# Attention and a multiplicative FFN on one Trainium2 core: q by 128 partitions with a tail, xT by pairs of batches, and x transposed by DMA from pair 10 on

## The chip, the core and the metric

The kernel runs on one core of a Trainium2 chip. A core has five engines that work side by side, each with its own in-order queue: TensorE (matmuls; PE in the profile, with its weight loads as PEld), VectorE (DVE), ScalarE (ACT), GpSimd (POOL) and SyncE (SP). Transfers and DMA transposes run on 16 DMA engines; an engine only issues them, and the issue stands in that engine's queue. The metric is device time in microseconds (us), less is better.

## The reference

Two stages, in float32 outside, for 8 batches, 8 heads, 1152 positions and head size 64:

```python
q_pool = q.reshape(B, H, S // factor, factor, D).mean(axis=3)      # factor 2: 576 queries a head
scores = scale * np.matmul(q_pool, k.transpose(0, 1, 3, 2))
attn = softmax(scores)                                             # over 1152 keys
x = (attn @ v).transpose(0, 2, 1, 3).reshape(B * 576, 512)         # 4608 tokens of 8 heads x 64
a = x @ w1                                                         # 512 x 1024
b = x @ w2
out = ((a * b) @ w3) @ w_out                                       # 1024 x 1024, 1024 x 512
```

Order of queries within a head is free inside the kernel, as long as each output row lands in its place.

## The kernel before

**Pairs.** Two heads of one batch are worked together as a pair; there are 32 pairs, four a batch. For each pair k, v and q are loaded in float32 (`load_kq`, L175, and `load_v`, L183). `cast_kq` (L189) makes 16-bit k on POOL and adds neighbouring queries (L198) on POOL too (on DVE for pair 0). q lies on 96 partitions by 6 queries each (`QP`, `QC`), k on 128 by 9.

**Turning k and q.** The scores need k and q with the head size on partitions. For pairs 0 to 7 `transp_pe` (L215) does it on TensorE: six transposes of q (L221), nine of k (L224), and three copies out on DVE. From pair 8 on `transp` (L207) issues two DMA transposes on SyncE (L210 for k into `kT2`, L212 for q into `qpT`).

**Scores and exponentials.** Keys by queries of a pair are a flat row of 9 x 576 columns, and all pairs form one long row, cut in 324 pieces of 512 columns. `scores` (L231) makes a piece for both heads with matmuls on L240 into one of three PSUM buffers `psc`, and ScalarE puts its exponential into a ring in SBUF (L245).

**Attention times v, and x.** A pair's queries are five tiles of 128 (the last one overlaps the one before by 64, `TO`). `av_pair` (L252) multiplies the ring by v with a column of ones for the sum: 18 matmuls (L259) into `avb`. `av_norm` (L274) takes the reciprocal (L276) and scales (L284) on DVE. The FFN needs x with features on partitions (`xT`, a ring of 5 batches of 576 tokens). For pairs below `XD` = 20 each tile is turned on TensorE (`x_turn`, L289, one transpose) and copied out by DVE (`x_copy`, L296); this happens one tile later, right behind the next tile's L259. From pair 20 on the five tiles are kept in `xb5`, and `x_dma` (L265) issues two DMA transposes on SyncE (L269 for four tiles, L271 for the last 64 queries).

**FFN.** The tokens are cut in 9 chunks of 512. w3 and w_out are first multiplied into one matrix (`t_groups`). `moe_groups` (L358) then gives a chunk 16 projections (L345, four matmuls of 512 columns each, alternately w1 and w2, with DVE multiplying the two on L370) and four output groups (L377, eight matmuls). The outputs are scaled and stored by `store` (L348), on POOL's queue while attention runs and on SyncE's after it. As positions in a chunk are tokens in 96-blocks, one group of 128 rows goes out in two or more transfers. The very last group is `go_last` (L393): it makes its 512 columns in two halves (L399), each scaled on ScalarE (L401), and is stored from ScalarE's queue.

**The order.** It is written out by the loop at L510 and nothing reorders it on an engine. A visit is three pieces of scores, one or two attention-value steps, and up to two FFN groups taken from a queue of chunks (`fill`): two projections or one output group with one step, one projection with two steps. There are 108 visits. At a pair's first piece the k and q transposes of the next pair are issued (`transp`) and the pair after that is prepared (`prepare`, L457: cast, then loads on SyncE's queue for pairs from 8 on, on POOL's before). A chunk enters the queue when its last x tile is there: `done_at` (L475) tells the attention-value step after which that is. For tiles turned on TensorE that is at once. For those turned by DMA the chunk is held until `HELD` = 5 steps past the end of the pair (L497). After the visits the remaining chunks are worked in the order in which they became ready, with ScalarE taking a part of the copies (`tail`).

Of the kernel before, what the change touches and what calls it, by code (L numbers as in the profile page):

```python
# [23 lines left out]
def _general(tc, q, k, v, out, w1sb, w2sb, T16):  # L24
# [8 lines left out]
    NF = dff // 128  # L33
    QP = 96
    QC = Sq // QP
    SCALE = 0.5 * float(D) ** -0.5
# [3 lines left out]
    with tc.tile_pool(name="gen", bufs=1) as sb, \  # L40
# [3 lines left out]
        for h in range(H):  # L44
# [70 lines left out]
def kernel(  # L115
# [20 lines left out]
    HP = H // 2  # L136
# [2 lines left out]
    G = 512  # L139
    NS = NP * FLAT // G  # L140
    RING = 24 * Sq
    QP = 96
    QC = Sq // QP
    E1 = D + 1
    SCALE = 0.5 * float(D) ** -0.5
    SCL = 16.0
    TO = [0, 128, 256, 384, Sq - 128]
    NT5 = len(TO)
# [6 lines left out]
    att = fast.enter_context(tc.tile_pool(name="att", bufs=2))  # L155
# [3 lines left out]
    ident16 = const.tile([128, 128], FP16)  # L159
# [13 lines left out]
    kq, vs, pairs = {}, {}, {}  # L173

    def load_kq(p, k_eng, q_eng):  # L175
        b, h0 = p // HP, 2 * (p % HP)
        kst = att.tile([128, 2, NJ * D], FP32, tag="kst")
        k_eng.dma_start(out=kst, in_=k[b, h0:h0 + 2].rearrange("u (p c) d -> p u (c d)", p=128))
        qst = att.tile([QP, 2, QC * 2 * D], FP32, tag="qst")
        q_eng.dma_start(out=qst, in_=q[b, h0:h0 + 2].rearrange("u (p c) d -> p u (c d)", p=QP))  # L180
        kq[p] = (kst, qst)

    def load_v(p, eng):  # L183
        b, h0 = p // HP, 2 * (p % HP)
# [2 lines left out]
        vs[p] = vst  # L187

    def cast_kq(p):  # L189
        kst, qst = kq.pop(p)  # L190
# [3 lines left out]
        qs = att.tile([QP, QC, 2, D], FP16, tag="qs")  # L194
        qv = qst.rearrange("p u (c t d) -> p u c t d", t=2, d=D)
        eng = nc.vector if p == 0 else nc.gpsimd
        for u in range(2):
            eng.tensor_tensor(out=qs[:, :, u, :], in0=qv[:, u, :, 0, :], in1=qv[:, u, :, 1, :], op=ALU.add)  # L198
        pairs[p] = [kpair, qs]

    def cast_v(p):
        va = vaugs[p % NVA]
# [2 lines left out]
        nc.gpsimd.tensor_copy(out=va[:, :, :, 0:D], in_=vs.pop(p).rearrange("p u (c d) -> p u c d", d=D))  # L205

    def transp(p):  # L207
        kpair, qs = pairs[p]
        kT2 = att.tile([128, NJ, 128], FP16, tag="kT2", bufs=3)
        nc.sync.dma_start(out=kT2, in_=kpair.rearrange("p c u d -> p (c u d)"), transpose=True)  # L210
        qpT = att.tile([128, QC, QP], FP16, tag="qpT", bufs=3)
        nc.sync.dma_start(out=qpT, in_=qs.rearrange("p c u d -> p (c u d)"), transpose=True)  # L212
        pairs[p] = (kT2, qpT.rearrange("p c i -> p (c i)"))

    def transp_pe(p):  # L215
        kpair, qs = pairs[p]
        kT2 = att.tile([128, NJ, 128], FP16, tag="kT2", bufs=3)
        qpT = att.tile([128, QC, QP], FP16, tag="qpT", bufs=3)
# [6 lines left out]
        nc.vector.tensor_copy(out=qpT.rearrange("p c i -> p (c i)"), in_=pt[:, 0:Sq])  # L225
        nc.vector.tensor_copy(out=kT2[:, 0:3].rearrange("p c i -> p (c i)"), in_=pt[:, Sq:Sq + 384])
        nc.vector.tensor_copy(out=kT2[:, 3:NJ].rearrange("p c i -> p (c i)"), in_=pt[:, 1024:1024 + (NJ - 3) * 128])  # L227
        pairs[p] = (kT2, qpT.rearrange("p c i -> p (c i)"))


    def scores(s):  # L231
# [16 lines left out]
    XR = 5 * Sq  # L248
    xT = att.tile([128, NC, XR], FP16, tag="xT", bufs=1)
    xbts = {}  # L250

    def av_pair(i):  # L252
        p, t = i // NT5, i % NT5
        va = vaugs[p % NVA]
        o = (i % 3) * 2 * E1
        for jt in range(NJ):
            c0 = ((p * NJ + jt) * Sq) % RING + TO[t]
            for u in range(2):
                nc.tensor.matmul(avb[:, o + u * E1:o + u * E1 + E1], ring[:, u, c0:c0 + 128], va[:, u, jt, :],  # L259
                                 start=(jt == 0 and u == 0), stop=(jt == NJ - 1), skip_group_check=True)  # L260

    XD = 20
    xb5 = {}

    def x_dma(p):  # L265
        b, hp = p // HP, p % HP
        c0 = (b * Sq) % XR
        xb = xb5.pop(p)
        nc.sync.dma_start(out=xT[:, hp, c0:c0 + 512].rearrange("p (t i) -> p t i", i=128),  # L269
                          in_=xb[:, 0:4].rearrange("p t u d -> p (t u d)"), transpose=True)  # L270
        nc.sync.dma_start(out=xT[:, hp, c0 + 512:c0 + Sq],  # L271
                          in_=xb[Sq - 512:128, 4].rearrange("p u d -> p (u d)"), transpose=True)
# [61 lines left out]
    CH = 512  # L334
# [23 lines left out]
    def moe_groups(c):  # L358
        gT = msb.tile([128, NF, CH], FP16, tag="g8", bufs=2, name="gT")
# [76 lines left out]
    def w_load(dst, src):  # L436
# [7 lines left out]
        out=ident16, in_=ident16, compare_op=ALU.not_equal, fill=1.0,  # L444
# [172 lines left out]
```

## Time and profile before

| | |
|---|---|
| median of 3 runs | 430.56 us (430.50 to 430.72) |
| profiled execution, its time | 430.84 us |
| its span, first to last instruction | 428.8 us |
| TensorE clock granted | 0.998 of full |
| TensorE busy | 408.0 us, 95% of the span |
| ScalarE busy | 326.7 us, 76% |
| VectorE busy | 205.5 us, 48% |
| GpSimd busy | 178.7 us, 42% |
| DMA moved | 84.59 MB in 79537 packets, 53489 of them under 512 B |
| attention's visits | about 11 to 350 us; the FFN alone after 364 us |

Groups in the profile have the line of the kernel, the engine, the operation, what it writes and reads, how often, then busy time and mean duration of one in ns, then the engine's idle time just before them and what ended most of it. Durations of matmuls are longer than their spacing, since they overlap in the array; starts are what to subtract. An engine with a "q" behind its name (SPq, POOLq, ACTq) is its queue issuing a transfer. The chain is the work that ended last, followed back from the end of the kernel.

### The profile page before, as it was taken

To read this page: it belongs to the slowest core of one execution; us is meant where nothing else is said; L and a number is where in the kernel's file an instruction comes from. 1 tells how busy PE (TensorE), PEld (TensorE's weight loads), DVE (VectorE), ACT (ScalarE), POOL (GpSimd) and SP (SyncE) were. 2 spreads that over 40 slices of the span, in tenths; PEclk is the share of its full clock that TensorE was granted. 3 is DMA by queue.
4 is the path that set the end of the run, shared out by engine and by line. 5 is a ranking of instruction groups with operands and counts; after the bars stand their busy time and mean duration, and the time that the engine had idled before them with its cause. 6 is when DMAs were issued, how large, how long until landed. Compare 5 with 4: busy or idle time off the path is not lost.

```text
span 428.8 us, 12736 instructions
## 1 busy us (share of the span) xinstructions
PE 408.0 (95%) x5317; PEld 251.2 (59%) x5317; DVE 205.5 (48%) x626; ACT 326.7 (76%) x359; POOL 178.7 (42%) x215
## 2 busy tenths in 40 slices
PE   1799999999999999999999999999999999999993
PEld 1376666666565656665666656665677856444442
DVE  1144564666356554655465635554445536534330
ACT  1889788889988988999889998999999980232221
POOL 3776755744675317630684218431861021000000
PEclk9999999999999999999999999999999999999999
DMA  8999999999999996999699949999795023030303
GB/s 254 250 262 264 251 232 229 264 230 239 276 296 289 256 216 205 278 232 270 178 252 280 307 100 240 254 252 240 216 205 108 15 64 69 10 99 0 99 1 105
DMA packets 79537, 84.59 MB, mean 197 GB/s; under 512 B 53489, under 2 KB 54513, under 8 KB 79473
## 3 DMA queue, kind: packets, MB, share of 16 engines
q1 hardware_dynamic: 70080, 56.57, 57.0%
q0 software_dynamic: 8544, 25.11, 23.7%
q10 hardware_dynamic: 848, 2.03, 1.7%
q8 instruction: 43, 0.70, 0.7%
q14 instruction: 22, 0.17, 0.1%
HBM read 67.11 MB, written 9.44 MB: 179 GB/s over the span
## 4 chain that ended last, share of the span: by engine, by line
PE 92%; DVE 3%; ACT 2%; DMA 2%; issue 0%; POOL 0%; ACTq 0%
PE avb L259 21%; PE psc L240 18%; PE mot L345 16%; PE mo L345 14%; PE mo L377 10%; PE mot L377 5%; PE mo L324 3%; ACT ring L245 2%; DMA kst<-in_k_dram 2%; PE avb L289 1%; PE ptk L224 1%; PE ptk L221 1%; DVE qpT L225 1%; PE mol L399 0%; PE mot L324 0%; DVE kT L227 0%
## 5 line engine op out<-in xcount | busy, mean ns | idle before, releaser
L245 ACT ACTIVATE ring<-psc 128x1024 f16<-128x1024 f32 x324 | 308.0, 1025 | 41.7 <-PE psc L240 38.7
L259 PEld LDWEIGHTS <-ring 128*128 128x128 f16 x2880 | 104.4, 98 | 36.5 <-issue 11.8
L259 PE MATMUL avb<-vaug,ring 128*128 128x65 f16 x2880 | 114.1, 193 | 2.1 <-DVE xT L296 1.4
L240 PE MATMUL psc<-qpT,kT 64*128 64x512 f16 (+7 forms) x1152 | 94.9, 291 | 2.8 <-ACT ring L245 1.8
L355 POOL DMA_DIRECT2D out_dram<-osb x48 | 25.1, 526 | 105.9 <-DVE rzall L276 105.8
L198 POOL TENSOR_TENSOR qs<-qst 96x384 f16<-96x384 f32 x62 | 60.5, 996 | 13.9 <-DMA qst<-in_q_dram 12.4
L240 PEld LDWEIGHTS <-kT 64*128 64x128 f16 x1152 | 45.5, 95 | 29.6 <-issue 6.1
L192 POOL CAST kpair<-kst 128x1152 f16<-128x1152 f32 x32 | 37.1, 1158 | 53.0 <-DMA kT<-kpair 22.5
L276 DVE RECIPROCAL rzall<-avb 128x2 f32<-128x2 f32 x160 | 26.6, 166 | 46.3 <-PE avb L289 30.8
L345 PEld LDWEIGHTS <-w2sb 128*128 128x128 f16 x320 | 28.6, 97 | 27.0 <-issue 2.8
L345 PEld LDWEIGHTS <-w1sb 128*128 128x128 f16 x320 | 28.4, 98 | 27.3 <-issue 3.4
L377 PEld LDWEIGHTS <-gT 128*128 128x128 f16 x280 | 25.5, 98 | 31.2 <-issue 4.0
L377 PE MATMUL mo<-T,gT 128*128 128x512 f16 x184 | 43.7, 380 | 0.0
L345 PE MATMUL mot<-xT,w2sb 128*128 128x512 f16 (+2 forms) x172 | 41.1, 364 | 0.0
L370 DVE TENSOR_TENSOR gT<-mot,asb 128x512 f16<-128x512 f32 x40 | 27.7, 692 | 24.2 <-PE mot L345 24.2
L205 POOL CAST vaug<-vst 128x1152 f16<-128x1152 f32 x32 | 36.6, 1145 | 6.1 <-DMA vst<-in_v_dram 6.0
L345 PE MATMUL mot<-xT,w1sb 128*128 128x512 f16 (+2 forms) x152 | 38.0, 373 | 0.0
L365 ACT COPY asb<-mot 128x512 f32<-128x512 f32 x21 | 12.3, 586 | 32.6 <-PE mot L345 32.6
L345 PE MATMUL mo<-xT,w1sb 128*128 128x512 f16 (+2 forms) x168 | 36.1, 344 | 0.0
L390 DVE TENSOR_SCALAR osb<-mo 128x512 f32<-128x512 f32 x23 | 15.9, 692 | 42.1 <-PE mo L377 42.1
L367 DVE COPY asb<-mo 128x512 f32<-128x512 f32 x35 | 24.2, 691 | 23.7 <-PE mo L345 23.7
L345 PE MATMUL mo<-xT,w2sb 128*128 128x512 f16 (+2 forms) x148 | 33.0, 351 | 0.0
(57 smaller groups left out, 266.8 us busy)
## 6 DMA issues: line engine op xcount, KB each, us to landing
vst<-in_v_dram SPq DMA_DIRECT2D x25, 576.0 KB, 6.2
kst<-in_k_dram SPq DMA_DIRECT2D x23, 576.0 KB, 6.9
qst<-in_q_dram SPq DMA_DIRECT2D x22, 576.0 KB, 8.1
kst<-in_k_dram POOLq DMA_DIRECT2D x8, 576.0 KB, 11.9
qst<-in_q_dram POOLq DMA_DIRECT2D x8, 576.0 KB, 13.6
vst<-in_v_dram POOLq DMA_DIRECT2D x7, 576.0 KB, 7.8
out_dram<-osb POOLq DMA_DIRECT2D x16, 192.0 KB, 3.4
w3c<-in_moe_w_dram POOLq DMA_DIRECT2D x4, 512.0 KB, 9.2
```

Of the source, the lines that this page charges most:

```text
L192: nc.gpsimd.tensor_copy(out=kpair.rearrange("p c u d -> p u c d"), in_=kst.rearrange("p u (c d) -> p u c d", d=D))
L198: eng.tensor_tensor(out=qs[:, :, u, :], in0=qv[:, u, :, 0, :], in1=qv[:, u, :, 1, :], op=ALU.add)
L205: nc.gpsimd.tensor_copy(out=va[:, :, :, 0:D], in_=vs.pop(p).rearrange("p u (c d) -> p u c d", d=D))
L240: nc.tensor.matmul(psc[:, u, f - s * G:f - s * G + ln], kT2[u * 64:u * 64 + 64, jt, :], qpT[u * 64:u * 64 + 64, i0:i0 + ln], start=True, s ...
L245: nc.scalar.activation(out=ring[:, :, r0:r0 + G], in_=psc, func=AF.Exp, bias=0.0, scale=SCALE)
L259: nc.tensor.matmul(avb[:, o + u * E1:o + u * E1 + E1], ring[:, u, c0:c0 + 128], va[:, u, jt, :], start=(jt == 0 and u == 0), stop=(jt == N ...
L276: nc.vector.reciprocal(out=rzall[:, i, :], in_=av[:, :, D:E1].rearrange("p u o -> p (u o)"))
L345: nc.tensor.matmul(pw[:, d0:d0 + n], wt[:, mc, ft * 128:ft * 128 + 128], xT[:, mc, a:a + n], start=(mc == 0 and d0 == 0), stop=(mc == NC - ...
L355: eng.dma_start(out=dst, in_=osb[r:r + n, :])
L367: nc.vector.tensor_copy(out=asb, in_=pa)
L370: nc.vector.tensor_tensor(out=gT[:, ft, :], in0=pb, in1=asb, op=ALU.mult)
L377: nc.tensor.matmul(po, gT[:, ft, tt:tt + 128], T16[:, ft, :], start=(ft == 0), stop=(ft == NF - 1))
```

## The change

Three things, which hang together by the block size of 128:

- q of a pair is loaded as 128 partitions by 4 queries (`qst`) plus the last 64 queries on 64 partitions (`qtl`), in two transfers; it is added in two instructions, and turned in 4 + 1 transposes on TensorE (pairs 0 to 7) or by two DMA transposes (from pair 8 on).
- `xT` holds the batches two by two: 4 blocks of 128 of the even batch, the 64 last queries of both side by side, 4 blocks of 128 of the odd batch (`xpos`). A group of 128 output rows is then one block of one batch, stored in one transfer, or the two tails, stored in two. Which step a chunk waits for follows from `xpos`.
- `XD` is 10 instead of 20: x of pairs 10 to 19 is turned by DMA too.

```diff
-    QP = 96
-    QC = Sq // QP
+    QM = 4
+    QT = Sq - QM * 128
...
-        qst = att.tile([QP, 2, QC * 2 * D], FP32, tag="qst")
-        q_eng.dma_start(out=qst, in_=q[b, h0:h0 + 2].rearrange("u (p c) d -> p u (c d)", p=QP))
+        qst = att.tile([128, 2, QM * 2 * D], FP32, tag="qst")
+        qtl = att.tile([QT, 2, 2 * D], FP32, tag="qtl")
+        q_eng.dma_start(out=qst, in_=q[b, h0:h0 + 2, 0:QM * 256].rearrange("u (p c) d -> p u (c d)", p=128))
+        q_eng.dma_start(out=qtl, in_=q[b, h0:h0 + 2, QM * 256:S].rearrange("u (p t) d -> p u (t d)", t=2))
...
-        for u in range(2):
-            eng.tensor_tensor(out=qs[:, :, u, :], in0=qv[:, u, :, 0, :], in1=qv[:, u, :, 1, :], op=ALU.add)
+        eng.tensor_tensor(out=qs.rearrange("p c u d -> p u c d"), in0=qv[:, :, :, 0], in1=qv[:, :, :, 1], op=ALU.add)
+        eng.tensor_tensor(out=qt, in0=qtl[:, :, 0:D], in1=qtl[:, :, D:2 * D], op=ALU.add)
...
-        qpT = att.tile([128, QC, QP], FP16, tag="qpT", bufs=3)
-        nc.sync.dma_start(out=qpT, in_=qs.rearrange("p c u d -> p (c u d)"), transpose=True)
+        qpT = att.tile([128, Sq], FP16, tag="qpT", bufs=3)
+        nc.sync.dma_start(out=qpT[:, 0:QM * 128].rearrange("p (c i) -> p c i", i=128),
+                          in_=qs.rearrange("p c u d -> p (c u d)"), transpose=True)
+        nc.sync.dma_start(out=qpT[:, QM * 128:Sq], in_=qt.rearrange("p u d -> p (u d)"), transpose=True)
...
-        for c in range(QC):
-            nc.tensor.transpose(pt[:, c * QP:c * QP + QP], qs[:, c].rearrange("p u d -> p (u d)"), ident16[0:QP, 0:QP])
+        for c in range(QM):
+            nc.tensor.transpose(pt[:, c * 128:c * 128 + 128], qs[:, c].rearrange("p u d -> p (u d)"), ident16)
+        nc.tensor.transpose(pt[:, QM * 128:Sq], qt.rearrange("p u d -> p (u d)"), ident16[0:QT, 0:QT])
...
+    def xpos(b, t):
+        if b % 2 == 0:
+            return b * Sq + t * 128
+        return b * Sq + (QT + t * 128 if t < QM else 0)
...
-    XD = 20
+    XD = 10
...
+        c0 = xpos(b, 0) % XR
+        nc.sync.dma_start(out=xT[:, hp, c0:c0 + QM * 128].rearrange("p (t i) -> p t i", i=128),
+                          in_=xb[:, 0:QM].rearrange("p t u d -> p (t u d)"), transpose=True)
+        c0 = xpos(b, QM) % XR
+        nc.sync.dma_start(out=xT[:, hp, c0:c0 + QT],
+                          in_=xb[128 - QT:128, QM].rearrange("p u d -> p (u d)"), transpose=True)
...
     def store(eng, pos, osb):
-        r = 0
-        while r < 128:
-            b, a = (pos + r) // Sq, (pos + r) % Sq
-            cc, p0 = a // QP, a % QP
-            n = min(QP - p0, 128 - r)
-            dst = out[b * Sq:b * Sq + Sq, :].rearrange("(p c) n -> p c n", c=QC)[p0:p0 + n, cc, :]
-            eng.dma_start(out=dst, in_=osb[r:r + n, :])
-            r += n
+        b, r = pos // (2 * Sq) * 2, pos % (2 * Sq)
+        if r == QM * 128:
+            for u in range(2):
+                r0 = (b + u) * Sq + QM * 128
+                eng.dma_start(out=out[r0:r0 + QT, :], in_=osb[u * QT:u * QT + QT, :])
+            return
+        if r > QM * 128:
+            b, r = b + 1, r - QM * 128 - 2 * QT
+        eng.dma_start(out=out[b * Sq:b * Sq + QM * 128, :].rearrange("(p c) n -> p c n", c=QM)[:, r // 128, :], in_=osb)
...
-        b, r = ((c + 1) * CH - 1) // Sq, ((c + 1) * CH - 1) % Sq
-        done_at.setdefault((b * HP + HP - 1) * NT5 + min(r // 128, NT5 - 1), []).append(c)
+        last = max((b * HP + HP - 1) * NT5 + t for b in range(B) for t in range(NT5)
+                   if xpos(b, t) < (c + 1) * CH and xpos(b, t) + (128 if t < QM else QT) > c * CH)
+        done_at.setdefault(last, []).append(c)
```

By this the last step that a chunk waits for moves by 1 to 4 steps for chunks 1, 3, 5 and 7 (chunk 7 now waits for the last tile of the last pair), and chunk 8 becomes ready one step earlier than chunk 7, so that the two change places in the order.

More of the change, by code (lines that the diff above doesn't have):

```diff
@@ L178, in load_kq @@
         k_eng.dma_start(out=kst, in_=k[b, h0:h0 + 2].rearrange("u (p c) d -> p u (c d)", p=128))
-        qst = att.tile([QP, 2, QC * 2 * D], FP32, tag="qst")
-        q_eng.dma_start(out=qst, in_=q[b, h0:h0 + 2].rearrange("u (p c) d -> p u (c d)", p=QP))
-        kq[p] = (kst, qst)
+        qst = att.tile([128, 2, QM * 2 * D], FP32, tag="qst")
+        qtl = att.tile([QT, 2, 2 * D], FP32, tag="qtl")
+        q_eng.dma_start(out=qst, in_=q[b, h0:h0 + 2, 0:QM * 256].rearrange("u (p c) d -> p u (c d)", p=128))
+        q_eng.dma_start(out=qtl, in_=q[b, h0:h0 + 2, QM * 256:S].rearrange("u (p t) d -> p u (t d)", t=2))
+        kq[p] = (kst, qst, qtl)
     def load_v(p, eng):
@@ L189, in cast_kq @@
     def cast_kq(p):
-        kst, qst = kq.pop(p)
+        kst, qst, qtl = kq.pop(p)
         kpair = att.tile([128, NJ, 2, D], FP16, tag="kpair")
@@ L193, in cast_kq @@
                               in_=kst.rearrange("p u (c d) -> p u c d", d=D))
-        qs = att.tile([QP, QC, 2, D], FP16, tag="qs")
+        qs = att.tile([128, QM, 2, D], FP16, tag="qs")
+        qt = att.tile([QT, 2, D], FP16, tag="qt")
         qv = qst.rearrange("p u (c t d) -> p u c t d", t=2, d=D)
         eng = nc.vector if p == 0 else nc.gpsimd
-        for u in range(2):
-            eng.tensor_tensor(out=qs[:, :, u, :], in0=qv[:, u, :, 0, :], in1=qv[:, u, :, 1, :], op=ALU.add)
-        pairs[p] = [kpair, qs]
+        eng.tensor_tensor(out=qs.rearrange("p c u d -> p u c d"), in0=qv[:, :, :, 0], in1=qv[:, :, :, 1], op=ALU.add)
+        eng.tensor_tensor(out=qt, in0=qtl[:, :, 0:D], in1=qtl[:, :, D:2 * D], op=ALU.add)
+        pairs[p] = [kpair, qs, qt]
     def cast_v(p):
@@ L207, in transp @@
     def transp(p):
-        kpair, qs = pairs[p]
+        kpair, qs, qt = pairs[p]
         kT2 = att.tile([128, NJ, 128], FP16, tag="kT2", bufs=3)
         nc.sync.dma_start(out=kT2, in_=kpair.rearrange("p c u d -> p (c u d)"), transpose=True)
-        qpT = att.tile([128, QC, QP], FP16, tag="qpT", bufs=3)
-        nc.sync.dma_start(out=qpT, in_=qs.rearrange("p c u d -> p (c u d)"), transpose=True)
-        pairs[p] = (kT2, qpT.rearrange("p c i -> p (c i)"))
+        qpT = att.tile([128, Sq], FP16, tag="qpT", bufs=3)
+        nc.sync.dma_start(out=qpT[:, 0:QM * 128].rearrange("p (c i) -> p c i", i=128),
+                          in_=qs.rearrange("p c u d -> p (c u d)"), transpose=True)
+        nc.sync.dma_start(out=qpT[:, QM * 128:Sq], in_=qt.rearrange("p u d -> p (u d)"), transpose=True)
+        pairs[p] = (kT2, qpT)
     def transp_pe(p):
-        kpair, qs = pairs[p]
+        kpair, qs, qt = pairs[p]
         kT2 = att.tile([128, NJ, 128], FP16, tag="kT2", bufs=3)
-        qpT = att.tile([128, QC, QP], FP16, tag="qpT", bufs=3)
+        qpT = att.tile([128, Sq], FP16, tag="qpT", bufs=3)
         pt = ps.tile([128, 2, 512], FP32, tag="psc", bufs=3, name="ptk").rearrange("p b c -> p (b c)").bitcast(FP16)
-        for c in range(QC):
-            nc.tensor.transpose(pt[:, c * QP:c * QP + QP], qs[:, c].rearrange("p u d -> p (u d)"), ident16[0:QP, 0:QP])
+        for c in range(QM):
+            nc.tensor.transpose(pt[:, c * 128:c * 128 + 128], qs[:, c].rearrange("p u d -> p (u d)"), ident16)
+        nc.tensor.transpose(pt[:, QM * 128:Sq], qt.rearrange("p u d -> p (u d)"), ident16[0:QT, 0:QT])
         cols = [Sq + c * 128 if c < 3 else 1024 + (c - 3) * 128 for c in range(NJ)]
@@ L224, in transp_pe @@
             nc.tensor.transpose(pt[:, cols[c]:cols[c] + 128], kpair[:, c].rearrange("p u d -> p (u d)"), ident16)
-        nc.vector.tensor_copy(out=qpT.rearrange("p c i -> p (c i)"), in_=pt[:, 0:Sq])
+        nc.vector.tensor_copy(out=qpT, in_=pt[:, 0:Sq])
         nc.vector.tensor_copy(out=kT2[:, 0:3].rearrange("p c i -> p (c i)"), in_=pt[:, Sq:Sq + 384])
         nc.vector.tensor_copy(out=kT2[:, 3:NJ].rearrange("p c i -> p (c i)"), in_=pt[:, 1024:1024 + (NJ - 3) * 128])
-        pairs[p] = (kT2, qpT.rearrange("p c i -> p (c i)"))
+        pairs[p] = (kT2, qpT)
     def scores(s):
@@ L266, in x_dma @@
         b, hp = p // HP, p % HP
-        c0 = (b * Sq) % XR
         xb = xb5.pop(p)
[L269 to L272, printed above, removed]
+        c0 = xpos(b, 0) % XR
[4 more added lines that the diff above has]
+                          in_=xb[128 - QT:128, QM].rearrange("p u d -> p (u d)"), transpose=True)
     def av_norm(i):
@@ L293, in x_copy @@
         b, hp = p // HP, p % HP
-        r0 = 0 if t < NT5 - 1 else NT5 * 128 - Sq
-        c0 = (b * Sq + TO[t] + r0) % XR
+        r0 = 0 if t < QM else 128 - QT
+        c0 = xpos(b, t) % XR
         nc.vector.tensor_copy(out=xT[:, hp, c0:c0 + 128 - r0], in_=xpt[:, r0:128])
```

## The prediction

> **What bounds the kernel now.** I read the page's busy times and chain first, then the rows by operation, then the order in time on TensorE, on SyncE and at the end.
>
> ```profile
> span 428.8 us, 12736 instructions
> ...
> PE 408.0 (95%) x5317; PEld 251.2 (59%) x5317; DVE 205.5 (48%) x626; ACT 326.7 (76%) x359; POOL 178.7 (42%) x215
> ...
> PE 92%; DVE 3%; ACT 2%; DMA 2%; issue 0%; POOL 0%; ACTq 0%
> ...
> L245 ACT ACTIVATE ring<-psc 128x1024 f16<-128x1024 f32 x324 | 308.0, 1025 | 41.7 <-PE psc L240 38.7
> ```
>
> TensorE carries 92% of the chain. ScalarE waits for it (38.7 us), but not by much: its 324 exponentials take 308.0 us, 0.95 us each, so a visit of three has a floor of 2.85 us. Both must be looked at visit by visit. First a visit while x is still turned on TensorE, then one after, both with two attention-value steps (V) and one projection (f):
>
> ```profile
> 167.16 0.83 PE L240 MATMUL psc<-qpT,kT 64*128 64x512 f16 x10
> 167.94 0.71 PE L259 MATMUL avb<-vaug,ring 128*128 128x65 f16 x18
> 168.49 0.22 PE L289 MATMUL avb<-ident,xbt 128*128 128x128 f16 x1
> 168.54 1.03 PE L345 MATMUL mo<-xT,w1sb 128*128 128x512 f16 x4
> 169.43 0.72 PE L259 MATMUL avb<-vaug,ring 128*128 128x65 f16 x18
> 169.99 0.22 PE L289 MATMUL avb<-ident,xbt 128*128 128x128 f16 x1
> 170.14 0.26 PE L240 MATMUL psc<-qpT,kT 64*128 64x192 f16 x2
> ```
>
> ```profile
> 270.74 0.87 PE L240 MATMUL psc<-qpT,kT 64*128 64x512 f16 x10
> 271.54 0.72 PE L259 MATMUL avb<-vaug,ring 128*128 128x65 f16 x18
> 272.10 1.02 PE L345 MATMUL mo<-xT,w1sb 128*128 128x512 f16 x4
> 272.96 0.71 PE L259 MATMUL avb<-vaug,ring 128*128 128x65 f16 x18
> 273.61 0.26 PE L240 MATMUL psc<-qpT,kT 64*128 64x192 f16 x2
> ```
>
> Columns: start, duration. From first score to first score: 170.14 - 167.16 = 2.98 us with two transposes (L289), 273.61 - 270.74 = 2.87 without. So before, this kernel already shows the state that the change extends: its visits from pair 20 on.
>
> **The change, part by part.** Sums are against the profiled execution: 430.84 us, of which 428.8 is span; the median of the three runs, 430.56, is 0.28 lower. No change that can be told is within 0.2%, 0.86 us.
>
> 1. *x by DMA from pair 10.* Fifty transposes on L289 and fifty copies on L296 go, in visits 39 to 71 (I number visits by three scores each). An L289 costs TensorE less than its 0.22 us, since matmuls overlap: in the rows above an L259 group's start lies 0.71 us ahead of the next score with L289 between (169.43 to 170.14) and 0.65 without (272.96 to 273.61). So it adds 0.06, and 50 x 0.06 = 3.0 us is the most if nothing else limits. I read it from whole visits: VfV takes 2.96 us early (17 visits, 2.95 to 2.98) and 2.88 late; two projections and one V 3.20 and 3.19; an output group (L377) and one V 3.20 and 3.155; with two V 3.81 and 3.69. Visits 39 to 71 are 14, 11, 5 and 3 of these: 14 x 0.084 + 11 x 0.016 + 5 x 0.045 + 3 x 0.125 = 1.96. Bounds -3.0 and -1.2 (only the VfV visits gain); I take **-2.0**, because late visits are the same instructions. The DVE copies cost nothing (DVE 48% busy).
>
> 2. *A later start of a chunk.* Chunk 2 was ready right after its last transpose; with DMA it is held until five V steps past the pair's end. By the order of issue that the code gives, visit 48 then finds no projection, and up to visit 71 two are done less (14 VfV, 10 with two projections and one V, 6 and 2 with an output group, and one empty); they come back in visits 90 and 105, one more each. A visit with two V and nothing else stood in the trace before:
>
> ```profile
> 67.77 0.83 PE L240 MATMUL psc<-qpT,kT 64*128 64x384 f16 x10
> ...
> 70.73 0.39 PE L240 MATMUL psc<-qpT,kT 64*128 64x512 f16 x2
> ```
>
> 2.96 us, as long as with a projection. So visit 48 saves almost nothing against a VfV; I give it the floor of 2.85. The visits to 71 then sum to 14 x 2.88 + 10 x 3.19 + 6 x 3.155 + 2 x 3.69 + 2.85 = 101.4 us, 0.8 below the 102.1 that term 1 leaves (104.1 - 2.0). Two projections of four matmuls, 0.216 us each, come later at full price, 1.73: **+0.9**. Bounds: +0.2 if TensorE ran through the empty visit (0.78 + 2 x 0.65 us), +1.0 by the row above.
>
> 3. *The end.* Chunk 8 now becomes ready one step before chunk 7 and is worked first. The split last group (`go_last`, L399) keys on chunk 8, so it moves into the middle and the kernel ends with an ordinary group of chunk 7.
>
> ```profile
> 419.96 1.04 PE L399 MATMUL mol<-T,gT 128*128 128x256 f16 x8
> 421.51 1.03 PE L399 MATMUL mol<-T,gT 128*128 128x256 f16 x8 [0.52 <-ACT osb L401]
> ```
>
> In the middle it holds TensorE 419.96 to 422.4, 2.42 us, against 8 x 0.216 = 1.73: +0.69. At the end, before: last store issued on ACT's queue at 423.40, landed 3.2 later, 6.6 us after the group's start. An ordinary group of chunk 6 starts at 378.51, its second store is issued at 381.74 and lands in 2.0: 5.2 us. So -1.35, net **-0.7**. Bounds: +0.7 (stores no earlier) and -1.4 (no wait in the middle).
>
> 4. *q.* On TensorE's pairs 0 to 7, six transposes of 96 columns (0.042 us warm, 0.080 in pairs 0 and 1) become four of 128 (0.056 and 0.107 by L224) and one of 64: at most **+0.15** in all. POOL: two adds of 996 ns for 384 elements become one of 512 and one of 128: by elements 1.33 + 0.33, from above 2.0, so -0.3 or 0 a pair; and an issue more of some 0.65 us in pairs 2 to 9. Nothing: k of pairs 3 to 7 is cast 8 us or more before its transposes. If that were gone, TensorE would wait for each late us. At the start, ACT's queue issues qst, qtl, then the next k; q landed at 6.79, the adds ended 7.83, six transposes were done 0.34 us before k's (8.90). qtl's bytes were part of qst's, so I take 0; if it landed only with the next k, 10.7, the start would move 2 us. Stores: 27 instead of 48 on POOL, 13 instead of 24 in the tail, hidden.
>
> 5. *SyncE's queue and the DMAs.* Each pair from 10 to 19 adds two transposes (1.2 and 1.12 us of SyncE's time); each from 8 on a q tail's transpose (about 1.1 by the 64-row one of x), each load of q one more issue (0.33). The tightest place is the transposes of pair 16, which now stand behind x of pair 12:
>
> ```profile
> 168.97 1.50 SPq L210 DMA_TRANSPOSE kT<-kpair  x1
> 170.52 2.34 SPq L212 DMA_TRANSPOSE qpT<-qs  x1
> ```
>
> q landed 7.6 us after issue, at 178.1; first use is 185.4, so 7.3 us of cover. x of pair 12 can be issued when its last V is scaled, about 168.7 in visit 48 (which starts 0.6 sooner than 167.16; then 0.78 of scores, 0.65 of V, 0.65 of DVE). Two issues put kT at 171.1, 2.1 later; the tail adds 1.1; the use comes 1.2 earlier: 2.9 us of cover left. Before, pair 29 had 4.2 in the same pattern and no wait. At pair 8, 1.3 us of cover (91.81 + 7.3 against 100.4), the added tail is issued at about 94.5, four us before kT has landed, so it lands with it. Loads: q's 96-partition transfer lands in 8.1 us, k's of 128 partitions and the same bytes in 6.9, so q may land sooner; it is hidden, as cover. I take **0**; from above, the longest landing of a transpose (12.0 against 7.6) at pair 16 alone gives +1.5, and +0.3 in each of 16 pairs +5.
>
> A rule speaks against this part. The Trainium skill, "DMA: Bandwidth & Descriptors", section "Rules for kernel authors", says to coalesce small transfers: under 64 KB one pays mostly overhead. The trace agrees (a 64-row x transpose holds SyncE 1.12 us, the one of 512 rows 1.2); by this rule the sum is unchanged while the cover holds and becomes that of the slower rival when it doesn't.
>
> Sum: -2.0 + 0.9 - 0.7 + 0.15 + 0 = **-1.65**, 429.2 in the profiled execution, **428.9** against the median.
>
> **The rivals.**
>
> *ScalarE is already the bound* (no difference). Late VfV visits, 2.82 to 2.97, sit at the floor 2.85. If all visits stayed at their early length, term 1 falls away and term 2 stays: 430.56 + 0.9 - 0.7 + 0.15 = 430.9; with half of term 1, 429.9. For it: late exponentials run nine in 8.65 us without a gap. Against: early visits of 2.96 to 3.2 are above the floor, and late ones with the same work are shorter. The Trainium skill, "Perfetto Trace Analysis", section "Identifying the Most-Contended Engine", holds matmul busy share a bad measure and weighs TensorE by its weight loads, here 59% against ScalarE's 76%; by this the rival is right, but the chain's 92% and the visits disagree.
>
> *SyncE's queue comes late* (slower). One mechanism: in-order SyncE waits for x, and behind it stand the transposes that the next scores need, at pair 16 first. From 2.9 us of added lateness on, each further us is a us of TensorE; with +0.3 a pair from 14 to 29, 430.56 + 4.8 - 1.65 = 433.7; with one stall of 4 us, 432.9. It ends slower than before from 1.65 us of waits on. For it: DMA engines are busy nine tenths and more until 300 us, and the transposes took up to 12 us to land. Against: from pair 20 on the pattern runs without a wait on TensorE.
>
> *The whole transpose is gained* (faster): TensorE's 3.0 fully, and term 2 by half: -3.0 + 0.45 - 0.7 + 0.15 = -3.1, 427.5. Against: the 2.85 floor.
>
> **How the numbers follow.** Forecast 0.56 (428.0 to 429.7); whole gain 0.08; ScalarE bound 0.18; late queue 0.18. Predicted 428.9. Range 427.6 to 431.6: it takes in the forecast, the ScalarE case and most of the whole gain, and leaves out the late queue past one small stall. The forecast's own range is 428.0 to 429.7. Faster 0.64 (forecast and whole gain), same 0.17, slower 0.19 (late queue and a little of the ScalarE case).
>
> **What would show it.** Right: L289 x50, visits 39 to 71 of 2.88 and 3.15 us; in visit 48 an exponential-paced 2.85 with TensorE waiting; L399 some 20 us before the end and the last store about 5.2 us after its group's start. Wrong: waits of L240 for kT or qpT between 160 and 240 us, or at pair 8; SyncE busy throughout; a first exponential later than 11.5 us; two-V visits still at 2.96.

## The result, and the profile after

The changed kernel takes **444.88 us** (median of 6 runs, 441.84 to 447.06) against 430.64 of the kernel before (6 runs beside them): ratio 1.0332, 95% interval 1.0292 to 1.0373. The forecast was 428.9 us, faster, with 431.6 as the upper end. It was wrong in sign. The runs of the changed kernel differ among themselves by 5.2 us, those of the kernel before by 1.0, so a difference of a few microseconds between two kernels with a full queue is read from their visits below and not from their times.

The profiled execution takes 446.48 us with a span of 444.3, against 430.84 and 428.8. The page of the changed kernel, with the rows that answer to those of before (busy shares, granted clock in forty slices, the chain of waits by engine and by line):

```profile
span 444.3 us, 12682 instructions
...
PE 411.4 (93%) x5259; PEld 252.2 (57%) x5259; DVE 199.4 (45%) x576; ACT 326.4 (73%) x359; POOL 165.4 (37%) x202
...
PEclk9999999999999999999999999996999999999997
...
PE 81%; DMA 10%; DVE 4%; ACT 2%; issue 1%; DVEq 0%; ACTq 0%
PE avb L271 18%; PE psc L246 16%; PE mot L358 14%; PE mo L358 12%; DMA xT<-xb 9%; PE mo L391 8%; PE mot L391 5%; PE mo L337 3%; ACT ring L251 2%; PE ptk L230 1%; DMA qst<-in_q_dram 1%; PE ptk L226 1%; DVE qpT L231 1%; PE avb L302 1%; DVE xb L297 1%
```

Every engine has fewer instructions or as many as before, and only TensorE's busy time is longer (411.4 us against 408.0), and yet the span grows by 15.4. The chain says where to look: TensorE's share falls from 92% to 81%, and DMA's rises from 2% to 10%, nearly all of it the transposes of x. The waits of the same kernel (who waits for whom: us in total, times, longest):

```profile
POOL kpair L194 <- DMA kT<-kpair: 50.0, 11, 7.3
...
DVE xb L297 <- DMA xT<-xb: 11.8, 7, 3.7
...
PE avb L271 <- DVE xb L297: 8.5, 8, 3.5
```

DVE waits to scale the x of a pair until the transfer of the pair two before it has left its buffer, and TensorE waits for DVE. DVE's wait is new: in the kernel before no wait of DVE for xT is among those named, and TensorE waits for DVE's xb there for 0.6 us in all. (POOL's wait in the first row stood before too, with 22.5 us; it is not in the chain.)

To see when it happened, I put the start of each visit (three scores) beside that of before; only differences are given, after minus before:

| stretch | us |
|---|---|
| start to visit 24 (pairs 0 to 7, q turned on TensorE) | +1.72 |
| visits 24 to 72 (x by DMA from pair 10 on) | -1.47 |
| visits 72 to 93 | +10.01 |
| visits 93 to 107 | +1.18 |
| visit 107 to the last matmul (72.63 and 72.62 us) | -0.01 |
| last matmul to the end of the span (6.27 and 10.27 us) | +4.00 |

They sum to 15.4, the difference of the spans. So there are three separate losses, and the gain that was forecast stands among them in visits 24 to 72. The run x_only below, which has the new x and the old q, tells the large loss from the rest: against it the changed kernel is 1.98 us late at every visit from 24 to 66, and 12.22 us late from 92 to 107. The large loss is thus 10.2 us and lies between visits 66 and 92. The +1.18 of visits 93 to 107 is no loss of its own: x_only has the same 1.18 there, projections that come back (term 2).

**The large loss: SyncE's queue.** SyncE's issues, one pair from k's transpose to the next x (start, duration), first in the kernel before, then after the change:

```profile
237.19 1.30 SPq L210 DMA_TRANSPOSE kT<-kpair  x1
238.55 1.93 SPq L212 DMA_TRANSPOSE qpT<-qs  x1
...
241.71 0.42 SPq L180 DMA_DIRECT2D qst<-in_q_dram  x1
249.28 1.20 SPq L269 DMA_TRANSPOSE xT<-xb  x1
```

```profile
239.88 2.09 SPq L213 DMA_TRANSPOSE kT<-kpair  x1
242.03 1.87 SPq L215 DMA_TRANSPOSE qpT<-qs  x1
243.95 1.22 SPq L217 DMA_TRANSPOSE qpT<-qt  x1
245.26 0.53 SPq L188 DMA_DIRECT2D vst<-in_v_dram  x1
245.89 0.41 SPq L178 DMA_DIRECT2D kst<-in_k_dram  x1
246.40 0.42 SPq L181 DMA_DIRECT2D qst<-in_q_dram  x1
246.91 0.69 SPq L182 DMA_DIRECT2D qtl<-in_q_dram  x1
247.69 1.25 SPq L281 DMA_TRANSPOSE xT<-xb  x1
```

Before, SyncE stands free from 242.13 to 249.28. After, each issue begins some 0.09 us after the one before it has ended. The reader is to look for the gap that isn't there: from 180 to 300 us SyncE's rows sum to 112.6 us, the small gaps to 8.3, and no gap is longer than 0.44 us. In the kernel before the rows sum to 73.9 us, and in gaps longer than half a microsecond SyncE stands free for 37.7 us. From 180.86 us, the issues of x follow each other at 11.3 us a pair (11 pairs in 124.6 us), while TensorE without waits needs 10.4 (157.0 us for visits 39 to 90 of the run x_only below, at 3.375 visits a pair). The queue falls behind by nearly a microsecond a pair, and the cover of k and q, from landed to first use, shows it: 15.2 us at pair 8, 8.5 at 12, 6.9 at 16, 2.5 at 19, -0.6 at 24. Before, it did not run down: 1.3 at pair 8, 7.3 at 16, 11.2 at 20, 10.7 at 24. The largest single stall stands at 303 us (last column: idle time before, and what ended it):

```profile
303.05 1.15 PE L271 MATMUL avb<-vaug,ring 128*128 128x65 f16 x18 [3.50 <-DVE xb L297]
```

The same 18 matmuls take 0.71 elsewhere; after the stall they take 1.15, and the granted clock of that slice is the lone 6 in the row above: it was 0.50 from 301.74 to 308.56 us. An estimate of the parts of the 10.2 us: TensorE's waits for xb are 8.5 us, of which x_only has 1.2 too, so 7.3; one wait for q's tail 0.2; and 5.5 us of work at half the clock, 303.05 to 308.56, which costs 2.8. They make 10.3.

**The small loss early.** q and k of one pair turned on TensorE, before, and then after:

```profile
41.38 0.42 PE L221 MATMUL ptk<-ident,qs 96*128 96x96 f16 x6
41.63 0.67 PE L224 MATMUL ptk<-ident,kpair 128*128 128x128 f16 x9
```

```profile
42.07 0.38 PE L226 MATMUL ptk<-ident,qs 128*128 128x128 f16 x4
42.39 0.20 PE L227 MATMUL ptk<-ident,qt 64*128 64x64 f16 x1
42.52 0.68 PE L230 MATMUL ptk<-ident,kpair 128*128 128x128 f16 x9
```

From the first transpose of q to the first of k it is 0.25 us before and 0.45 after. The four of 128 rows follow each other at 0.055; from the last of them to the one of 64 rows it takes 0.150, and from that to k's 0.131.

**The end.** The order of chunks 7 and 8 puts the split group in the middle, as forecast, and SyncE's last issues are now the two halves of the last tile, the two tails of 64 rows:

```profile
434.95 1.72 SPq L366 DMA_DIRECT2D out_dram<-osb  x2
```

They end at 436.67, and only behind them SyncE reads the flag for the general path (436.72), 2.7 us after the last matmul. Before it read it at 421.94, 0.6 us ahead of the last matmul, with the last stores on ScalarE's queue. Behind the flag come SyncE's branch and closing instructions, 6.9 us to the end before and 7.5 now.

### The profile page after: what moved, and what is told of

Its sections match the earlier page's. It is cut to its first block, busy times and chain, and to the rows that moved or that the text cites. A ratio compares the mean times of both kernels' runs of the same rounds, so it can differ in the third digit from the quotient of the medians.

```text
span 444.3 us, 12682 instructions
## 1 busy us (share of the span) xinstructions
PE 411.4 (93%) x5259; PEld 252.2 (57%) x5259; DVE 199.4 (45%) x576; ACT 326.4 (73%) x359; POOL 165.4 (37%) x202
## 2 busy tenths in 40 slices
DMA packets 91697, 86.07 MB, mean 194 GB/s; under 512 B 60656, under 2 KB 64752, under 8 KB 91632
## 4 chain that ended last, share of the span: by engine, by line
PE 81%; DMA 10%; DVE 4%; ACT 2%; issue 1%; DVEq 0%; ACTq 0%
PE avb L271 18%; PE psc L246 16%; PE mot L358 14%; PE mo L358 12%; DMA xT<-xb 9%; PE mo L391 8%; PE mot L391 5%; PE mo L337 3%; ACT ring L251 2%; PE ptk L230 1%; DMA qst<-in_q_dram 1%; PE ptk L226 1%; DVE qpT L231 1%; PE avb L302 1%; DVE xb L297 1%
## 5 line engine op out<-in xcount | busy, mean ns | idle before, releaser
L246 PE MATMUL psc<-qpT,kT 64*128 64x512 f16 (+7 forms) x1152 | 97.1, 293 | 3.1 <-ACT ring L251 1.8
L289 DVE RECIPROCAL rzall<-avb 128x2 f32<-128x2 f32 x160 | 26.4, 165 | 48.2 <-PE avb L271 32.1
L370 POOL DMA_DIRECT2D out_dram<-osb x21 | 11.6, 554 | 85.0 <-DVE rzall L289 71.2
L200 POOL TENSOR_TENSOR qs<-qst 128x512 f16<-128x512 f32 x31 | 39.4, 1272 | 5.1 <-DMA qpT<-qt 2.2
L358 PE MATMUL mot<-xT,w1sb 128*128 128x512 f16 (+2 forms) x168 | 40.1, 364 | 0.0
L391 PE MATMUL mo<-T,gT 128*128 128x512 f16 x168 | 39.9, 380 | 0.0
L297 DVE TENSOR_TENSOR xb<-avb,rzall 128x128 f16<-128x128 f32 x110 | 32.1, 291 | 15.4 <-DMA xT<-xb 11.8
L384 DVE TENSOR_TENSOR gT<-mot,asb 128x512 f16<-128x512 f32 x37 | 25.6, 692 | 28.1 <-PE mot L358 28.1
L358 PE MATMUL mot<-xT,w2sb 128*128 128x512 f16 (+2 forms) x152 | 38.0, 373 | 0.0
L379 ACT COPY asb<-mot 128x512 f32<-128x512 f32 x21 | 12.3, 586 | 33.3 <-PE mot L358 33.3
L358 PE MATMUL mo<-xT,w2sb 128*128 128x512 f16 (+2 forms) x168 | 36.3, 345 | 0.0
L384 DVE TENSOR_TENSOR gT<-mo,asb 128x512 f16<-128x512 f32 x35 | 24.2, 691 | 25.0 <-PE mo L358 25.0
## 6 DMA issues: line engine op xcount, KB each, us to landing
qst<-in_q_dram POOLq DMA_DIRECT2D x8, 512.0 KB, 10.3
```

What stands on the lines that cost most here:

```text
L200: eng.tensor_tensor(out=qs.rearrange("p c u d -> p u c d"), in0=qv[:, :, :, 0], in1=qv[:, :, :, 1], op=ALU.add)
L246: nc.tensor.matmul(psc[:, u, f - s * G:f - s * G + ln], kT2[u * 64:u * 64 + 64, jt, :], qpT[u * 64:u * 64 + 64, i0:i0 + ln], start=True, s ...
L289: nc.vector.reciprocal(out=rzall[:, i, :], in_=av[:, :, D:E1].rearrange("p u o -> p (u o)"))
L297: nc.vector.tensor_tensor(out=xbt, in0=av[:, :, 0:D], in1=rzall[:, i, :].unsqueeze(2).to_broadcast([128, 2, D]), op=ALU.mult)
L358: nc.tensor.matmul(pw[:, d0:d0 + n], wt[:, mc, ft * 128:ft * 128 + 128], xT[:, mc, a:a + n], start=(mc == 0 and d0 == 0), stop=(mc == NC - ...
L384: nc.vector.tensor_tensor(out=gT[:, ft, :], in0=pb, in1=asb, op=ALU.mult)
```

## The experiments

Three theories of the large loss. **Q**: SyncE's queue is the bound, because a pair's issues take longer than TensorE takes for a pair. **D**: the DMA engines are the bound, by the load of bytes and packets. **B**: the two buffers of xb5 are the bound, since the scaling of a pair waits for the transfers of the pair two before it. All times are medians beside runs of the kernel before on the same chip; its medians there were 430.79 (first four runs), 431.08 (next four) and 430.74 (last three).

**x alone** (the kernel before, x by DMA from pair 10 on):

```diff
-    XD = 20
+    XD = 10
```

> The kernel before with x by DMA from pair 10 and nothing else. Theory Q (SyncE's queue is the bound: after the change a pair needs nine issues, at least 0.53 + 0.41 + 0.42 + 0.62 + 1.22 + 1.11 + 1.3 + 1.25 + 1.22 = 8.1 us and nine gaps of 0.09, and 10.1 to 12.7 us as seen between 180 and 305 us, where TensorE takes 10.4 a pair): here seven issues, 6.2 us at least and some 8.5 with the same stretching, so the cover does not run down; waits of DVE for xT from before small, and the gain of the changed kernel's visits 39 to 66 (2.1 us) stays, less 0.9 for the projection that comes late: 429.3 us. Theory D (the DMA engines' throughput is the bound: 576 more rows of 256 B a pair): the rows are the same as in the changed kernel, so cover runs down as there and 8 to 10 us are lost between 240 and 310 us: 438.

429.97 us, ratio 0.9983 (0.9973 to 0.9993), near theory Q's 429.3 and far from D's 438. The part that was meant to gain does gain, a little. SyncE still stands free for 13.1 of the 120 us from 180 on; TensorE isn't held.

**q alone** (the changed kernel, x on TensorE until pair 20):

```diff
-    XD = 10
+    XD = 20
```

> The changed kernel with x by DMA from pair 20 as before. Both theories: TensorE's q transposes cost 1.7 us by the ninth pair as in the changed kernel (64-row transposes at 130 to 150 ns and 150 before them), the middle and the end 4.0 us (split group 0.65, SyncE's last stores and its fetch behind them 3.4), nothing is gained on x: 430.6 + 1.7 + 4.0 = 436.3. Theory Q: to pair 20 SyncE needs 6.7 us at least and some 8.5 stretched, so there is no wait before 250 us, and after it a run-down of up to 0.9 us a pair that the cover of 12 us absorbs: 436 to 437. Theory D: without the 576 rows the cover stays until 250 us, 436 to 438. It prices the q part; it does not tell the two apart.

434.17 us, ratio 1.0072 (1.0055 to 1.0089), 2.1 less than expected. In the profiled execution visits begin 1.6 us late from 24 until 92, so until x comes in at pair 20 there is no loss but the early one; from then on the cover runs down from 13.9 us at pair 19 to -1.1 at pair 28, and visits 93 to 102 lose 2.8 us. That execution took 437.62 us and the four others 434.07 to 434.28, so by their times most of this late loss is missing in them: with q alone the queue is near its limit behind pair 20. The two parts alone make -0.8 and +3.4; together they make +14.2. What they share is a queue that each alone leaves free time in (13.1 and 13.0 of the 120 us).

**Loads on POOL's queue** (the changed kernel):

```diff
-        eng = nc.gpsimd if early else nc.sync
+        eng = nc.gpsimd
```

> The changed kernel with all loads of k, q and v on POOL's queue for all pairs, not only the first eight; the same bytes and rows, only four issues a pair leave SyncE (0.53 + 0.41 + 0.42 + 0.62 = 2.0 us and 0.4 of gaps). Theory Q: SyncE's five transposes need 6.1 us at least, 8.5 stretched, so waits of DVE for xT and of the scores for qpT go, about 10 us: 435. Theory D: the DMA engines move the same, the cover runs down as before: 444 to 446. If POOL's stores and casts delay the loads (POOL waits up to 20 us for an output group), waits for kst or vst appear instead.

462.72 us, and the runs spread from 449 to 474. It settled nothing: SyncE has four issues a pair less, but those that stay get longer (one of k took 14.36 us, and transfers issued about then landed after some 20), and POOL's casts stand behind its waits for output groups. It only shows that POOL was no free place.

**The end** (the changed kernel, chunks in ascending order):

```diff
-    ready.extend(c for _, c in held)
+    ready.extend(sorted(c for _, c in held))
```

> The changed kernel with chunks 7 and 8 after the attention in their old order, so that the split last group and the store from ScalarE's queue are at the end again. My account of the end (SyncE must issue the last two stores, then read the flag, then fetch its closing code, 12.2 us from the last group's start to the end instead of 8.8; and the split group in the middle 0.65): 4.0 us less than the changed kernel, 440.9. The rival, that the end only looks longer because stores land later: no change, 444.9.

440.19 us, ratio 1.0228 (1.0189 to 1.0268), 4.7 us less than the changed kernel, where 4.0 was expected. From visit 107 to the last matmul it takes 72.63 us as in every kernel here, and from the last matmul to the end 6.16, as in the kernel before (6.27). So the end gives 4.1. In its profile the large loss is there too (visit 105 begins 7.2 us late, 10.6 in the changed kernel); up to there the two run the same instructions, and the 3.4 between them is a spread between runs, not the edit's.

**One transpose less** (the changed kernel; q's tail as a padded fifth block, on TensorE and on SyncE):

```diff
-        qs = att.tile([128, QM, 2, D], FP16, tag="qs")
-        qt = att.tile([QT, 2, D], FP16, tag="qt")
+        qs = att.tile([128, QM + 1, 2, D], FP16, tag="qs")
+        nc.gpsimd.memset(qs[QT:128, QM], 0.0)
...
-        nc.sync.dma_start(out=qpT[:, 0:QM * 128].rearrange("p (c i) -> p c i", i=128),
-                          in_=qs.rearrange("p c u d -> p (c u d)"), transpose=True)
-        nc.sync.dma_start(out=qpT[:, QM * 128:Sq], in_=qt.rearrange("p u d -> p (u d)"), transpose=True)
+        nc.sync.dma_start(out=qpT.rearrange("p (c i) -> p c i", i=128),
+                          in_=qs.rearrange("p c u d -> p (c u d)"), transpose=True)
...
```

> The 64 queries become a fifth block of q's tile, padded with zeros to 128 partitions: one transposing DMA a pair in place of two (1.22 us of issue and a gap of 0.09 less on SyncE's queue, 16 KB more to transpose), and five 128-row transposes a pair on TensorE in place of four and one of 64 rows. Against 444.9 us for the changed kernel. Theory Q (SyncE's queue is the bound: a pair's issues and gaps, 11.3 us, are more than TensorE's 10.4): 10.0 us a pair fits again, the ten us lost in visits 78 to 92 go, the changed end and the chunk order stay: 434 us. Theory D (the load on the DMA engines is the bound): the bytes stay, 443 to 446. Theory B (the two buffers of xb5 are the bound): 442 to 445. Besides, if the 0.195 us a pair of the early part come from the change of 128 rows to 64 on TensorE, visit 24 starts at most 1.0 us later than before the change, not 1.72.

432.70 us, ratio 1.0043 (1.0026 to 1.0060): 12.2 us less, with more bytes to transpose and more packets in all (92464 against 91697): neither D nor B explains that. From visit 24 to 107 it loses and gains what x alone does (-0.54 and -0.52 us), so the whole of the large loss is gone. SyncE's queue of this kernel, for the same part of a pair as above:

```profile
242.22 1.31 SPq L213 DMA_TRANSPOSE kT<-kpair  x1
243.59 1.31 SPq L215 DMA_TRANSPOSE qpT<-qs  x1
...
247.62 0.62 SPq L182 DMA_DIRECT2D qtl<-in_q_dram  x1
248.34 1.23 SPq L280 DMA_TRANSPOSE xT<-xb  x1
```

6.1 us instead of 7.8, and SyncE is free for 12.1 of the 120 us. Cover stays at 5.8 us or more up to pair 28, and visits 72 to 90 are as long as before. The early loss goes too: q's five transposes of 128 rows take 0.28 us up to k's,

```profile
40.62 0.44 PE L226 MATMUL ptk<-ident,qs 128*128 128x128 f16 x5
40.90 0.67 PE L229 MATMUL ptk<-ident,kpair 128*128 128x128 f16 x9
```

so one transpose more of full height is cheaper than the change of height. The end is unchanged by this edit and still costs 8.76 us after the last matmul.

**Issue time almost without bytes** (x alone, with two 64-row transposes a pair more on SyncE, from a constant tile into tiles that nobody reads):

```diff
+    tin = const.tile([64, 128], FP16, name="tin")
+    nc.vector.memset(tin, 0.0)
+    touts = [const.tile([128, 64], FP16, name=f"tout{i}") for i in range(4)]
...
+        for u in range(2):
+            nc.sync.dma_start(out=touts[2 * (p % 2) + u], in_=tin, transpose=True)
...
-    XD = 20
+    XD = 10
```

> x by DMA from the eleventh pair with q as before (429.97 us), and from the ninth pair on two more transposing DMAs a pair on SyncE's queue, of 64 rows each from a constant tile into unused ones: 2.6 us of issue and gaps a pair, 32 KB. Theory Q: a pair's cycle on SyncE goes from 9.1 to 11.7 us, beyond TensorE's 10.4, the cover of some 5.5 us is used up in four or five pairs, and 1.3 us a pair is lost in what follows: 438 to 450 us. Theory D: 32 KB among some 1.7 MB a pair move nothing: 430 to 431. Theory B has no reason of its own for a loss here: 430 to 432.

457.50 us (its fourth run took 467.87), ratio 1.0621 (1.0600 to 1.0642), beyond even Q's range. 32 KB a pair cost some 27.5 us. SyncE has no free time from 180 to 300 us, and its issues of x follow each other at some 12.3 us; the chain:

```profile
PE 66%; DMA 26%; POOL 3%; DVE 1%; issue 1%; ACT 1%; ACTq 0%; DVEq 0%; SPq 0%; POOLq 0%
```

Bytes can't explain this, and packets hardly: there are 90544 of them, 5% more than in x alone. With the padded block above, theory D as the whole cause falls. What Q's price left out shows in the trace: TensorE waits 19.4 us for DVE's xb (1.2 in x alone), and after three of these waits its granted clock is 0.50, for 13.7 us in all; it is at work for 11.1 of them, which costs some 5.6 us (an estimate).

**Three buffers of x** (the changed kernel):

```diff
-                xb5[p] = att.tile([128, NT5, 2, D], FP16, tag="xb5", bufs=2, name="xb5")
+                xb5[p] = att.tile([128, NT5, 2, D], FP16, tag="xb5", bufs=3, name="xb5")
```

> The changed kernel with three buffers of xb5 in place of two, so that the scaling of pair p+3 and no longer that of p+2 waits for the transfers of pair p. Theory B: DVE's wait at L297 for the transfer and TensorE's behind it were the loss: 434 to 436 us. Theory Q and D: SyncE's queue is as late as before, and the wait moves to the scores, which then wait for kT and qpT: 441 to 446 us.

440.17 us, ratio 1.0217 (1.0200 to 1.0234): between the two, 4.7 less than the changed kernel (1.1 of it, by the profiles, before visit 24, where the edit does nothing). By the visits from 24 to 107, set against x alone, 4.2 us are lost, where the changed kernel loses 10.2 and its run with ascending chunks 7.6. The chain shows that the wait did move:

```profile
PE 85%; DMA 6%; DVE 3%; ACT 2%; issue 1%; SPq 0%; ACTq 0%; DVEq 0%
PE avb L271 19%; PE psc L246 17%; PE mot L358 15%; PE mo L358 13%; PE mo L391 8%; PE mot L391 6%; DMA qpT<-qs 4%; PE mo L337 3%; ACT ring L251 2%; PE ptk L230 1%; DMA qpT<-qt 1%; DMA qst<-in_q_dram 1%; PE ptk L226 1%; DVE w3T L331 1%; DVE qpT L231 1%; PE avb L302 1%
```

In place of 9% in xT it has 5% in q, and TensorE's waits for q are 3.7 us, those for xb 1.2 as in x alone. SyncE is as full (no free time), and cover still runs down to -1.8 us (pair 29). So the two buffers aren't the cause, but they are the place where a late queue bites first, and by these numbers they made it dearer.

**Bytes without issues** (the changed kernel, k and v of one head a pair loaded and used for both):

```diff
-        k_eng.dma_start(out=kst, in_=k[b, h0:h0 + 2].rearrange("u (p c) d -> p u (c d)", p=128))
+        k_eng.dma_start(out=kst, in_=k[b, h0:h0 + 1].rearrange("u (p c) d -> p u (c d)", p=128))
...
-        eng.dma_start(out=vst, in_=v[b, h0:h0 + 2].rearrange("u (p c) d -> p u (c d)", p=128))
+        eng.dma_start(out=vst, in_=v[b, h0:h0 + 1].rearrange("u (p c) d -> p u (c d)", p=128))
...
```

> The changed kernel with k and v loaded for one head of each pair only and used for both: it leaves out the keys and values of the odd heads, 576 KB of DMA a pair less, with as many issues. The smallest issues of a pair sum to 8.9 us with their gaps, 11.3 are seen; what stretches them is open. Theory Q in its pure form (the stretch is SyncE's own): 11 us a pair still, 441 to 446 us. Theory D (the stretch comes from the engines' load, and the cycle falls to 9.5 or less): the loss of visits 78 to 92 goes, 432 to 436 us.

434.65 us, ratio 1.0082 (1.0065 to 1.0099): the loss of visits 78 to 92 goes here as well, with as many issues as in the changed kernel. So Q's pure form falls too. What became shorter are the issues themselves, from 180 to 300 us: k's transpose takes 1.40 us in the mean instead of 2.21, q's main one 1.47 instead of 1.96; SyncE's rows and short gaps come to 9.7 us a pair, a little over the 9.5 expected, and it stands free for 6.2 of the 120 us. The two answers together: a pair costs SyncE a fixed 8.9 us in the changed kernel (the smallest of each issue, and nine gaps), and some 2.4 us of stretch that come with what the DMA engines have in hand; how the load makes an issue longer, these runs do not show. Neither alone is above TensorE's 10.4; the sum is. Taking away either was enough.

**Term 2 alone, and a better kernel.** If chunk 2's late start costs what was forecast, a shorter hold gives it back (x alone, with the one edit):

```diff
-    HELD = 5
+    HELD = 3
```

> x by DMA from the eleventh pair with q as before (429.97 us, 0.9983 of the kernel before), and HELD 3 in place of 5, so that chunk 2 comes into the plan before visit 48 has nothing to fill in. If the later start of chunk 2 is worth the 0.9 us of the second term: visit 48 lasts 0.85 us longer, visits 90 to 93 and 105 lose their extra projection each, 429.1 us, ratio 0.996. Rival: a projection so much earlier waits for the transfer of x, which lands 6.7 us after its issue: 430 us or more, with TensorE waiting for xT at the projections.

429.09 us, ratio 0.9965 (0.9954 to 0.9977), 0.9 less as expected; TensorE has no wait for a transfer of x. In the trace visit 48 is now 2.82 us, with its projection, only 0.09 longer than in x alone and not 0.85; but visits 36 to 72 together are 0.79 longer, and from visit 75 to 107 the lead of 1.3 us stays (in x alone, 2.65 shrinks to 0.78).

**All repairs together:** the padded block, the ascending order of chunks and HELD 3; and the same with XD = 8.

> The changed kernel with the 64 queries as a padded fifth block (432.7 us), the held chunks in ascending order, and HELD 3. By the account of the end (the time after the last matmul, 8.8 us, falls to the 6.3 of before): 2.5 us less; by the second term 0.9 us less: 429.3 us, ratio 0.996. If the end's cost lay in the transfers of the new store's layout and not in who issues it last: 431.8 us.

> The same with x by DMA from the ninth pair on. Two pairs more at 0.2 to 0.27 us each (the first term is 2.0 to 2.7 us for ten pairs): 0.5 us less, 428.8 us, ratio 0.995. Rival: SyncE's queue, which issues k and q for pairs 10 to 12 just then, loses cover: 429.3 to 431 us.

428.41 us, ratio 0.9941 (0.9928 to 0.9954), and 427.59 us, ratio 0.9924 (0.9911 to 0.9937). Both beat the kernel before, by less than 1%, and are somewhat better than expected. For the second a part of that is chance: the two profiled executions differ by 1.4 us, of which 0.8 is there by visit 24, where the kernels do the same, and only 0.3 comes from visits 24 to 36, where the two pairs more act. After the last matmul they need 5.70 and 5.40 us, SyncE is free for 10.6 and 13.0 of the 120 us, and the chain of the second is the kernel before's again:

```profile
span 424.9 us, 12681 instructions
...
PE 91%; DVE 3%; ACT 3%; DMA 1%; issue 0%; ACTq 0%
```

## Why the prediction was wrong, step by step

- **Term 1, x by DMA (-2.0): right.** With HELD 3, visits 36 to 72 gain 1.73 us in x_held3 (from 0.26 late to 1.47 early), and the same 1.73 in joined_sorted. It lies inside the bounds; the transposes on L302 are 50, as expected. *ScalarE already the bound*, the rival of no difference, falls with it, and so does *the whole transpose gained* (3.0). The weight-load share by which the Trainium skill, "Perfetto Trace Analysis", section "Identifying the Most-Contended Engine", would have put ScalarE first does not fit here: taking work from TensorE shortened these visits.
- **Term 2, chunk 2 later (+0.9): right.** Visit 48 took 2.73 us (2.85 was forecast), visits 90 and 105 took back one projection each (4.14 and 4.04 us in x alone, against 3.14 and 3.17), and HELD 3 gave 0.9 us.
- **Term 3, the end (-0.7): wrong, +4.0.** The step that failed is "an ordinary group of chunk 6 ... 5.2 us. So -1.35": it took a group from the middle and followed its stores, and left out what SyncE does behind them. The 0.52 us hold of the split group is the same at either place (72.63 us in both orders), so the +0.69 in the middle was given back. But SyncE issues the last two stores, for 1.7 us, and reads the flag behind them, and the time after the last matmul went from 6.27 us to 10.27. The ascending order brought 6.16. The same changed order needed only 8.8 in q_only and q_joined; there the flag is read at the same place (2.6 us after the last matmul), and what is missing is a second pause of some 1.4 us among SyncE's closing instructions, which the changed kernel, three buffers and one head of k and v have. What SyncE waits for there is not shown.
- **Term 4, q on TensorE (at most +0.15): wrong by size, 0.20 a pair.** The step is "four of 128 ... and one of 64", priced by columns. The change from 128 rows to 64 and back costs about 0.1 us each way. It stood in the rows that the prediction shows: from a transpose of x (L289, 128 rows) to the scores (L240, 64 rows) it is 0.15 (169.99 to 170.14), and to a projection of 128 rows 0.05 (168.49 to 168.54). Visits 6 to 24 gave +1.02 us; with five blocks of 128, +0.22. The Trainium skill, "TensorEngine Tiling (Array Packing)", section "Key Properties", says that a change of tiling mode drains TensorE, without a price. The trace fits this, though it does not show the drain itself: 0.150 instead of 0.055 us is the price here. The rest of the 1.72 at visit 24 was there by visit 6; kernels with this same start differ there by 1.0 us (-0.34 to +0.70), so I read nothing into it.
- **Term 5, SyncE's queue (0): wrong, +10.2, and the rival came true by half.** The failing step is "the tightest place is the transposes of pair 16": it asked whether one transfer would come in time, and it did, with 6.9 us of cover where 2.9 were computed. It never asked how long a pair's issues are in sum. From the rows of before, 180 to 300 us: k's transpose 1.77, q's 1.96, v, k and q 0.75, 0.55 and 0.39, x 1.42 and 1.28, with seven gaps of 0.09: 8.8 us. The forecast's own 1.1 and 0.33 for the tail, with two gaps, make that 10.4, TensorE's time for a pair, with nothing left; measured, the tail's two issues took 1.39 and 0.72. The argument against the rival, "from pair 20 on the pattern runs without a wait", was one of a pattern with seven issues a pair, not nine. The rival named the right queue and the right outcome, slower. Its mechanism was another: it had SyncE stand waiting for x and the scores wait for k and q behind it, where SyncE had no time left at all, and TensorE waited for the scaling of x into a buffer that was still to be transferred (8.5 us) and for k and q hardly (0.2). So of its signs, "SyncE busy throughout" came, and the waits of the scores did not; its price (433.7) was for a few late pairs, not for a queue that never catches up.
- **The rule** weighed against term 5, from the Trainium skill, "DMA: Bandwidth & Descriptors", section "Rules for kernel authors", to coalesce small transfers: the trace agrees. The 64-row transpose holds SyncE 1.22 us, the one of 640 rows that took its place together with the 512-row one 1.27 at least, and joining them was worth 12.2 us with the early part.

## What to carry to other kernels

Before adding issues to a queue, sum what one round of the loop costs that queue, at the durations the profile shows and with the gaps, and set it against the time of a round on the engine that bounds; a cover of many microseconds only says how many rounds it takes until the loss shows. Two edits that each leave some free time in the same queue can fail together, so price them together. And look at what the last queue to finish still has to do behind its last store.

## What the runs showed of the hardware

- A transposing DMA costs its queue much the same whatever its size: 1.1 us at least for x's 64 rows, 1.2 for q's 64 and for x's 512, 1.27 for k's 1152.
- An issue gets longer while the DMA engines have much in hand: k's transpose went from 1.40 us in the mean to 2.21 when k and v brought twice the bytes, with the same instructions around it (1.71 to 2.55 in the other kernels with all bytes).
- TensorE's change between operands of 128 rows and 64 rows costs 0.150 us where 0.055 is the pace, so that a padded block is cheaper than a short one.
- After a stall of 3.50 us TensorE's granted clock was 0.50 for 6.8 us (0.83 from 300 to 320 us, where x_only and q_joined show 1.00). The length of a stall alone does not decide it: in x_tiny stalls of 2.18, 3.40 and 4.83 us were followed by half clock and one of 3.35 us was not, nor was one of 2.84 us in the run with ascending chunks. The Trainium skill, "TensorE: Matmul & The Clock Gate", section "Part 1: The HAM clock gate", puts the fall to half clock at about 3.4 us of idleness; all of these stalls but that of 2.18 us agree with it, and for that one the measurement decides.
